# Logits and gate product at one place of a step, and five more weight blocks at the seam to the tail

## The chip, the cores and the metric

The kernel runs on one core of one Trainium2 chip. The metric is the device time of one execution in microseconds (us). The engines named below are PE (TensorE, matrix products; PEld is its weight load), DVE (VectorE), ACT (ScalarE), POOL (GpSimd) and SP (SyncE, which issues every DMA here).

## The reference

Three stages follow one another; everything is float32.

```
# 1 memory attention: 4 batches, 8 heads, 576 tokens, 64 wide, 32 memory slots
a    = softmax(phi, over tokens)                  # [4,8,576,32]
k_m  = a.T @ k ;  v_m = a.T @ v                   # [4,8,32,64]
attn = softmax(q @ k_m.T / 8) @ v_m
x    = attn, heads side by side                   # [2304,512]
# 2 experts weighted by domain: 4 experts, w1 512x1024, w2 1024x512
x    = sum_e p[:,e] * (relu(x @ w1[e]) @ w2[e])   # p = domain_probs, rows normalised
# 3 slots: 8 experts with 4 slots each
logits = x @ phi2                                 # [2304,32]
s    = softmax(logits, over tokens).T @ x         # 32 slot inputs
s    = relu(s[expert] @ v1[expert]) @ v2[expert]  # v1 512x1024, v2 1024x512
out  = softmax(logits, over slots) @ s
```

## The kernel before

The body never forms the 512-wide `x` of stage 2. Per batch it has attention weights `A` (two parts, high and low) and the product G of each head's `v_m` with `w1` (`g_mult`, L374 to L397). A hidden block is then G times A: `up()` (L424 to L449) is six matrix products of 128x128 by 128x288 (L435 to L437), a ReLU on ACT into a buffer `hT` (L445), and, after the last range of tokens, a transpose on DVE into `h` (L447). `logits()` (L451 to L472) multiplies `hT` by M, the product of `w2` and `phi2`, into the bank `lb`; its 128x32 products are line L469. `g_mult` has 64x32 products (L392), 16 of them per step into two of four PSUM banks called `at`; `g_out` (L399 to L403) takes each bank out by a cast on ACT (L402) and a subtraction on DVE (L403).

The work is cut into units: batches 0, 1 and 2 whole (two ranges of 288 tokens each), batch 3 in two halves (units 3 and 4). A unit has 8 steps n of 512 hidden columns. The 24 steps of units 0 to 2 and the two steps in which units 3 and 4 go together have eight `up` calls each (full steps); the other twelve have four. The order is written by hand: a loop over the `up` calls of a step (places 0 to 7) puts `logits` of the step before behind place `at_l`, `g_mult` of the next step behind `at_g`, `g_out` at the places `at_c`, and calls `pump()` at every place. `pump()` takes one item from the list `fg` and one from `bg`. `bg` holds the attention of a later batch. `fg` holds the stages of the unit that just ended, put there by `finish()`: `whole` (L575, L578, L579), `stats` (L586 to L594), `exps`, `weights(0)` and `weights(1)` (L615 and L617, which write `we`), then `sums` (L644, 32x32 products of `we` with `h`, into all four `at` banks; L652 or L654 adds them to `srun`), then row stages for the softmax over slots (L662 to L688). `None` in these lists is a place left empty.

The weights of stage 3 are 128x512 blocks of 256 KB, taken in one fixed order: 32 of `w2`, 64 of `v1`, 64 of `v2`. `fill` puts the next blocks into a buffer that has come free, and SP issues their DMAs, each after the one eight places ahead of it has landed. The seam is the stretch behind the last `up`: the last `logits`, `whole` to `weights` of unit 4, the last `sums`, with short products of the identity (`warm`, L790) between them that compute nothing. `warm2` takes a new `lb` bank for them. Behind the last `sums` the buffers `raw`, `g` and `A0`, which held `h` until then, take weight blocks, and the tail computes stage 3 from them.

Of the kernel before, what the change touches and what calls it, by code (L numbers as in the profile page):

```python
# [8 lines left out]
F32 = mybir.dt.float32  # L9
F32R = mybir.dt.float32r  # L10
ACTF = mybir.ActivationFunctionType
ALU = mybir.AluOpType
# [4 lines left out]
def kernel(  # L17
# [23 lines left out]
    nc = tc.nc  # L41
# [11 lines left out]
    pc = ctx.enter_context(tc.tile_pool(name="pc", bufs=1))  # L53
    hTp = ctx.enter_context(tc.tile_pool(name="hTp", bufs=5))
# [10 lines left out]
    def mbank():  # L65
        return psm.tile([128, 512], F32, tag="mm", name="mm")
# [13 lines left out]
    pe = const.tile([128, B, NT, E], F32)  # L80
# [280 lines left out]
    NU = len(units)  # L361
# [43 lines left out]
    hid, hT, half, joint = {}, {}, [None], {}  # L405

    def hid_tile(u, e):

        b, ranges = units[u]
        nt = (ranges[-1][1] - ranges[0][0]) // 32  # L410
        if u < NU - 2:
            hid[u, e] = big([128, nt, 8, 32], "h")
        elif u == NU - 2:
            if e % 2 == 0:
                half[0] = big([128, 2, nt, 8, 32], "h")
            hid[u, e] = half[0][:, e % 2]
        elif e == 0:
            hid[u, e] = const.tile([128, nt, 8, 32], F32, tag="A0", name="h")
        elif e < 3:
            hid[u, e] = rawp.tile([128, nt, 8, 32], F32, tag="raw", name="h")  # L420
        else:
            hid[u, e] = gp.tile([128, nt, 8, 32], F32, tag="g", name="h")
# [108 lines left out]
    def group(u):  # L531

        b, ranges = units[u]
        base, end = ranges[0][0], ranges[-1][1]
        w = end - base
        nt, tb0 = w // 32, base // 32
        st = {}

        def flat(t):
            return t.rearrange("p n s -> p (n s)")  # L540
# [56 lines left out]
        def exps():  # L597
# [9 lines left out]
                )  # L607
            st["zg"] = zg

        def weights(h):  # L610

            def f():
                if h == 0:
                    st["dt"] = pc.tile([128, nt, 32], F32, tag="lt", name="dt")
                    nc.vector.transpose(out=flat(st["dt"]), in_=flat(st["lc"]))  # L615
                we = st["we", h] = pc.tile([128, nt, 2, 32], F32, tag="we", bufs=2, name="we")
                nc.vector.tensor_tensor(  # L617
                    out=we, in0=st["dt"].unsqueeze(2).to_broadcast([128, nt, 2, 32]),
                    in1=pe[:, b, tb0:tb0 + nt, 2 * h:2 * h + 2].unsqueeze(3).to_broadcast(
                        [128, nt, 2, 32]  # L620
                    ), op=ALU.mult,
                )
                if h == 1:
                    nc.vector.tensor_copy(out=mrun, in_=st["mg"])
                    if st["first"]:
                        nc.vector.tensor_copy(out=zrun, in_=st["zg"])
                    else:
                        nc.vector.scalar_tensor_tensor(
                            out=zrun, in0=zrun, scalar=st["fo"], in1=st["zg"],
                            op0=ALU.mult, op1=ALU.add,  # L630
                        )
            return f
# [106 lines left out]
    def fill(pool, tag, n, again=True, **kw):  # L739

        n = min(n, len(order) - nxt[0])
        if n:
            t = pool.tile([128, n, 512], F32, tag=tag, name="v", **kw)
            keys = order[nxt[0]:nxt[0] + n]
            m = 0
            while m < n:
                m += fetch(t[:, m:n], n - m)
            left = [n]
            for key in keys:
                held[key] = (left, again, pool, tag, n, kw)  # L750
# [11 lines left out]
    with tc.manual_schedule():  # L762
# [14 lines left out]
            out=dp[:, 0:16, :].rearrange("p (b r) e -> p b (r e)", b=B),  # L777
# [7 lines left out]
        wb = [mbank()]  # L785

        def warm(n):

            for _ in range(n):
                nc.tensor.matmul(wb[0][:, 0:128], ident, ident, start=True, stop=True)  # L790
# [7 lines left out]
        for n in range(2):  # L798
            nc.gpsimd.memset(kbd[n], 0.0)
        nc.vector.tensor_reduce(  # L800
            out=si, in_=ident.rearrange("p (c s) -> p s c", c=4), axis=AX.X, op=ALU.add
        )
        for i in range(4):
            nc.vector.tensor_copy(out=rr[:, i, :], in_=si)
            nc.vector.tensor_copy(
                out=r2[:, i, :].rearrange("p (b i s) -> p b i s", b=2, i=4),
# [16 lines left out]
        def warm2(n):  # L823
            wb[0] = psl.tile([128, 512], F32, tag="lb", name="wb")
            warm(n)
# [12 lines left out]
            out=dp, in0=dp, in1=dps.unsqueeze(2).to_broadcast([128, 18, E]), op=ALU.mult  # L838
# [22 lines left out]
        fg, bg, heavy = [], [], []  # L861
# [13 lines left out]
        def attention(b, lead):  # L875
# [26 lines left out]
            return items  # L902

        groups = [group(u) for u in range(NU)]

        steps = [(n, (b,)) for b in range(B - 1) for n in range(NCH)]
# [4 lines left out]
        def finish(lu, n):  # L911

            _, g_, sums, rows = groups[lu]
            if lu < NU - 2:
                rw = [None] * 5 + [f for row in rows for f in (row, None, None)]
            else:
                rw = [f for row in rows for f in (row, None)]
            if lu < NU - 2:
                ps_ = [sums(k, 5) for k in range(5)] if lu < NU - 3 else [sums(k, 4) for k in range(4)]
                fg.extend([None] * 3 + g_[:2] + [None] + g_[2:5])  # L920
                fg.extend([None] * (2 if lu < NU - 3 else 3) + ps_ + rw)
            else:
                ps_ = [sums(k, 2) for k in range(2)]
                fg.extend([None] + g_[:5] + ps_ + [None] * 4 + rw)
            heavy[:] = [g_[0]] + ps_
            if lu < NU - 3:
                bg.extend([None] * 5 + attention(lu + 2, 5))

        for n, us in steps:
            b = units[us[0]][0]  # L930
            s = b * NCH + n
            ups = [
                (u, fb, ki) for fb in range(4) for u in us for ki in range(len(units[u][1]))
            ]
            if us == (0,) and n == 0:
                ups.sort(key=lambda x: x[2])

            if len(ups) == 8:
                at_l, at_g, at_c = 0, 2, (3, 4)
            elif n == MIX:  # L940
                at_l, at_g, at_c = 1, 2, (3,)
            else:
                at_l, at_g, at_c = int(us != (NU - 1,) or n > MIX), 0, (1, 2)
            if us == (0,) and n == 0:
                bg += attention(1, 4)
                bg.insert(12, shares)
            if n == 0 and us[0]:
                assert len(bg) == 0
            if n % 2 == 0:
                for u in us:  # L950
                    hid_tile(u, n // 2)
            if us == (NU - 2,) and n == MIX:
                fill(att, "ph", 2, again=False)
                fill(att, "kt", 1, again=False)
                fill(att, "q", 1, again=False, bufs=2)
            if us == (NU - 2,) and n == NCH - 1:
                fill(bigp, "big", 9)
            if us == (NU - 1,) and n == MIX:
                fill(gp, "g", 4)
                for _ in range(4):  # L960
                    fill(bigp, "big", 9)
            gs = []
            for at, (u, fb, ki) in enumerate(ups):
                up(u, n, fb, ki)
                if at in at_c and gs:
                    gs.pop(0)()
                    if us == (0,):
                        gs.pop(0)()
                if at == at_l:
                    for lu, ln in last:  # L970
                        logits(lu, ln)
                    for lu, ln in last:
                        if ln % 2:
                            groups[lu][0](ln // 2)
                        if ln == NCH - 1:
                            finish(lu, n)
                if at == at_g and s + 1 < NG and us != (NU - 1,):
                    gs = g_mult(s + 1)
                pump(not gs or at != at_g)
                if us == (0,):  # L980
                    for f in early[at] if n == 0 else ():
                        f()
                    if n and at in (1, 2, 3, 4, 6, 7):
                        ms[n][(1, 2, 3, 4, 6, 7).index(at) + 1]()
                    if at == 5 and n + 1 < NCH:
                        ms[n + 1][0]()
            for f in gs:
                f()
            last = [(u, n) for u in us]
# [2 lines left out]
        groups[lu][0](ln // 2)  # L992
        fill(const, "A1", 4, again=False)
        fill(const, "M", 2, again=False)

        g_ = groups[lu][1]
        warm2(8)
        g_[0]()
        for f in g_[1:]:
            f()  # L1000
        warm2(14)
        groups[lu][2](0, 1)()
        warm2(6)
        for _ in range(2):
# [30 lines left out]
        part = pc.tile([128, 512], F32, tag="acc", name="part")  # L1035
# [214 lines left out]
```

## Time and profile before

| | |
|---|---|
| time, median of 3 | 575.85 us (574.59 to 579.08) |
| the profiled execution: time / span / mean granted clock | 577.05 us / 575.3 us / 0.983 |
| PE busy | 532.0 us, 92% of the span |
| DVE busy | 288.6 us, 50% |
| ACT busy | 217.4 us, 38% |
| DMA | 106.24 MB, mean 185 GB/s |

A busy time is the sum over an engine's instructions, overlaps within the engine taken once. The granted clock is the share of full speed at which PE was run: 1.0 is 2.4 GHz. The body lasts to about 464 us of the span, the seam to about 486 us, and the tail is the rest.

### The profile page before, as it was taken

The numbers are of one execution on the slowest core, as the hardware profiler recorded it, in microseconds if no ns is written. First come the engines' busy times: TensorE is split into PE (matmuls) and PEld (weight loads), VectorE is DVE, ScalarE is ACT, GpSimd is POOL, SyncE is SP. The second block draws the span as 40 slices with busy tenths as digits, with TensorE's granted clock in tenths as the row PEclk, the third lists the DMA queues.
The fourth block names the chain that finished last, engine by engine and source line by source line (L and its number), as shares of the span: only waits on it lengthen the run. The fifth ranks groups of instructions, "written<-read, shape, count | busy, mean of one in ns | idle before, by whom it ended". The sixth has DMA issues, their size and how long they took to land.

```text
span 575.3 us, 15609 instructions
## 1 busy us (share of the span) xinstructions
PE 532.0 (92%) x6814; PEld 380.6 (66%) x6814; DVE 288.6 (50%) x612; ACT 217.4 (38%) x557; POOL 18.0 (3%) x31
## 2 busy tenths in 40 slices
PE   7989999999999899999999999998999987998983
PEld 7767777777776678867667887765676765333341
DVE  5546525544480756767256667753567461022022
ACT  2445555655551345545124455421343220011022
POOL 0000001001000010100000010000010010000000
PEclk9999999999999999999999999999999998899798
DMA  8995444444240844424067333241722597999997
GB/s 200 317 286 213 136 143 163 156 148 148 74 124 5 262 153 129 139 75 123 3 191 224 93 106 142 75 149 28 255 106 74 180 389 264 373 386 386 355 355 261
DMA packets 91492, 106.24 MB, mean 185 GB/s; under 512 B 29472, under 2 KB 54560, under 8 KB 91424
## 3 DMA queue, kind: packets, MB, share of 16 engines
q1 hardware_dynamic: 91424, 105.24, 56.3%
q8 instruction: 54, 0.88, 0.6%
q14 instruction: 14, 0.11, 0.1%
HBM read 100.50 MB, written 4.72 MB: 183 GB/s over the span
## 4 chain that ended last, share of the span: by engine, by line
PE 74%; DMA 10%; DVE 8%; issue 4%; ACT 3%; SPq 2%; POOL 0%; DVEq 0%; ACTq 0%; POOLq 0%
PE mm L435 12%; PE mm L437 10%; PE mm L436 9%; PE at L644 9%; PE lb L469 6%; PE at L392 5%; DMA v<-in_moe_w_dram 5%; PE mm L1195 4%; DMA raw<-in_moe_w_dram 3%; PE at L316 3%; PE at L496 2%; DVE g L403 2%; PE mm L790 2%; PE at L224 2%; PE at L300 1%
## 5 line engine op out<-in xcount | busy, mean ns | idle before, releaser
L445 ACT ACTIVATE hT<-mm 128x288 f32<-128x288 f32 x256 | 105.8, 414 | 206.3 <-PE mm L437 182.3
L447 DVE STREAM_TRANSPOSE h<-hT 128x576 f32<-128x576 f32 (+1 forms) x160 | 103.6, 652 | 150.5 <-ACT hT L445 137.9
L435 PE MATMUL mm<-A,g 128*128 128x288 f32 x512 | 167.2, 327 | 1.8 <-ACT g L402 1.0
L437 PE MATMUL mm<-A,g 128*128 128x288 f32 x512 | 151.5, 296 | 1.6 <-DVE g L403 1.6
L436 PE MATMUL mm<-A,g 128*128 128x288 f32 x512 | 151.1, 295 | 0.8 <-DVE A L353 0.8
L435 PEld LDWEIGHTS mm<-A,g 128*128 128x128 f32 x512 | 96.5, 189 | 46.0 <-issue 27.6
L437 PEld LDWEIGHTS mm<-A,g 128*128 128x128 f32 x512 | 96.2, 188 | 2.9 <-DVE g L403 2.9
L436 PEld LDWEIGHTS mm<-A,g 128*128 128x128 f32 x512 | 96.6, 189 | 1.2 <-DVE A L353 1.0
L644 PE MATMUL at<-h,we 32*32 32x256 f32 x2304 | 55.6, 394 | 6.7 <-issue 4.0
L644 PEld LDWEIGHTS at<-h,we 32*32 32x32 f32 x2304 | 33.6, 104 | 24.3 <-issue 9.2
L403 DVE TENSOR_TENSOR g<-at,g 128x512 fp32r<-128x512 f32 x64 | 41.7, 667 | 2.3 <-ACT g L402 2.2
L469 PE MATMUL lb<-hT,M 128*32 128x288 f32 x512 | 39.6, 413 | 0.2 <-ACT M L522 0.2
L392 PE MATMUL at<-raw,vb 64*32 64x512 f32 x512 | 35.7, 601 | 1.9 <-DMA raw<-in_moe_w_dram 1.5
L402 ACT CAST g<-at 128x512 fp32r<-128x512 f32 x64 | 36.4, 585 | 0.0
L1195 PE MATMUL mm<-v,hz 128*8 128x256 f32 x256 | 29.8, 415 | 4.1 <-DMA v<-in_moe_w_dram 3.5
L1195 PEld LDWEIGHTS mm<-v,hz 128*8 128x8 f32 x256 | 11.2, 93 | 21.1 <-DMA v<-in_moe_w_dram 9.9
L496 PE MATMUL at<-ident,w 128*128 128x128 f32 x128 | 20.0, 279 | 2.4 <-DVE g L403 2.4
L469 PEld LDWEIGHTS lb<-hT,M 128*32 128x32 f32 x512 | 13.1, 109 | 12.7 <-issue 5.6
L316 PEld LDWEIGHTS at<-kbd,qt 128*128 128x128 f32 (+1 forms) x160 | 17.8, 180 | 3.8 <-issue 3.0
L316 PE MATMUL at<-kbd,qt 128*128 128x64 f32 (+1 forms) x160 | 19.4, 264 | 0.2
L496 PEld LDWEIGHTS at<-ident,w 128*128 128x128 f32 x128 | 14.5, 141 | 6.5 <-DVE g L403 3.4
L1055 PE MATMUL mm<-v,sT 128*32 128x512 f32 x128 | 16.3, 653 | 1.1 <-DMA v<-in_moe_w_dram 0.8
(159 smaller groups left out, 489.8 us busy)
## 6 DMA issues: line engine op xcount, KB each, us to landing
raw<-in_moe_w_dram SPq DMA_DIRECT2D x32, 1024.0 KB, 5.2
v<-in_moe_w_dram SPq DMA_DIRECT2D x18, 1024.0 KB, 13.8
v<-in_moe_w_dram SPq DMA_DIRECT2D x46, 256.0 KB, 6.0
w<-in_moe_w_dram SPq DMA_DIRECT2D x16, 512.0 KB, 6.9
v<-in_moe_w_dram SPq DMA_DIRECT2D x10, 768.0 KB, 10.5
kv<-in_k_dram SPq DMA_DIRECT2D x8, 512.0 KB, 5.1
kv<-in_v_dram SPq DMA_DIRECT2D x8, 512.0 KB, 6.0
out_dram<-ot SPq DMA_DIRECT2D x16, 256.0 KB, 4.1
```

The source lines that it names most:

```text
L316: nc.tensor.matmul(sc[0:n, :, j, :], st["qt"][:, j, 0:n], kbd[b % 2][:, j], start=True, stop=True)
L392: nc.tensor.matmul(ts[c][32 * i:32 * i + 32, :], vb[b % 2][64 * c:64 * c + 64, 32 * i:32 * i + 32], raw[s][64 * c:64 * c + 64, i, :], star ...
L403: nc.vector.tensor_tensor(out=lo, in0=t, in1=hi.bitcast(F32), op=ALU.subtract)
L435: nc.tensor.matmul(ps, gh, ah, start=(c == 0), stop=False)
L436: nc.tensor.matmul(ps, gh, al, start=False, stop=False)
L437: nc.tensor.matmul(ps, gl, ah, start=False, stop=(c == 1))
L445: nc.scalar.activation(out=t[:, o0 - base:o1 - base], in_=ps, func=ACTF.Relu)
L447: nc.vector.transpose(out=hid[u, n // 2][:, :, 4 * (n % 2) + fb], in_=t[:, 0:o1 - base])
L469: nc.tensor.matmul(lb[0][p:p + 32, 0:o1 - o0], M[:, 4 * n + a, :], hT[u, n, a][:, o0 - base:o1 - base], start=start, stop=stop,)
L496: nc.tensor.transpose(t[:, 128 * c:128 * c + 128], st["w"][:, a, 128 * c:128 * c + 128], ident)
L644: nc.tensor.matmul(ts[p][32 * e:32 * e + 32, 0:256], st["we", e // 2][rows, tb, e % 2], hid[u, e][rows, tb].rearrange("p k f -> p (k f)"), ...
L1195: nc.tensor.matmul(accs[acc][32 * i:32 * i + 8, 0:256], hz[:, dh != 2, f, i, :], blk[:, 256 * m:256 * m + 256], start=(dh == 2 and f == 0) ...
```

## The change

- In 24 of the 26 full steps (not in steps 0 and 1 of unit 0) `logits` and `g_mult` both stand behind the second `up`, and the two parts of `g_out` at places 2 and 3.
- Of units 0 to 2 the stages from `whole` on begin one place earlier, and the first `sums` stand two places earlier than before in the list; counted in places of the step the first one is at place 4 instead of 5 (unit 2: 5 instead of 6). Of units 3 and 4 the row stages come two places earlier.
- The last unit writes its weights `we` in two halves of token tiles, both expert pairs of a half together.
- At the seam the five `hT` buffers take one weight block each, ahead of everything that `raw`, `g` and `A0` take.
- The `warm` products use a bank of `up`, not `lb`, and are 4 and 10, not 8 and 14.

```diff
+        def part(h, t0, n):
+            if t0 == 0:
+                st["we", h] = pc.tile([128, nt, 2, 32], F32, tag="we", bufs=2, name="we")
+            nc.vector.tensor_tensor(
+                out=st["we", h][:, t0:t0 + n],
...
         def weights(h):
...
-                we = st["we", h] = pc.tile([128, nt, 2, 32], F32, tag="we", bufs=2, name="we")
-                nc.vector.tensor_tensor(
...
+                if u < NU - 1:
+                    part(h, 0, nt)
+                else:
+                    for g in range(2):
+                        part(g, 5 * h, 5 if h == 0 else nt - 5)
...
-                fg.extend([None] * 3 + g_[:2] + [None] + g_[2:5])
-                fg.extend([None] * (2 if lu < NU - 3 else 3) + ps_ + rw)
+                fg.extend([None] * 2 + g_[:2] + [None] + g_[2:5])
+                fg.extend([None] * (1 if lu < NU - 3 else 2) + ps_ + rw)
...
-                fg.extend([None] + g_[:5] + ps_ + [None] * 4 + rw)
+                fg.extend([None] + g_[:5] + ps_ + [None] * 2 + rw)
...
-                at_l, at_g, at_c = 0, 2, (3, 4)
+                at_l, at_g, at_c = (0, 2, (3, 4)) if us == (0,) and n < 2 else (1, 1, (2, 3))
...
         fill(const, "M", 2, again=False)
+        for _ in range(5):
+            fill(hTp, "hT", 1, again=False)
...
-        warm2(8)
+        wb[0] = mbank()
+        warm(4)
...
-        warm2(14)
+        wb[0] = mbank()
+        warm(10)
```

The order of instructions, as the program issues them. On PE, in a full step of unit 0 during which another batch's attention runs (L224 to L263 are its work), before:

```order
L437 MATMUL mm<-A_97,g 128x288
L469 MATMUL lb<-hT,M 32x288 x8
L244 MATMUL at<-ind,sm 128x1
L248 MATMUL at<-ind,ph 128x1
L244 MATMUL at<-ind,sm 128x1
L248 MATMUL at<-ind,ph 128x1
L435 MATMUL mm<-A_97,g 128x288
...
L392 MATMUL at<-raw,vb_101 32x512 x8
L263 MATMUL at<-ident,km 128x128
```

and now:

```order
L437 MATMUL mm<-A_97,g 128x288
L469 MATMUL lb<-hT,M 32x288 x8
L392 MATMUL at<-raw,vb_101 32x512 x8
L244 MATMUL at<-ind,sm 128x1
L248 MATMUL at<-ind,ph 128x1
L244 MATMUL at<-ind,sm 128x1
L248 MATMUL at<-ind,ph 128x1
L435 MATMUL mm<-A_97,g 128x288
```

L469 and L392 were two interruptions of the `up` products and are one.

On DVE, in step 1 of unit 1, where unit 0's weights are written and its first sums follow (in the changed kernel the weights are line L614 for L617, `mrun` and `zrun` L634 and L636), before:

```order
L617 TENSOR_TENSOR we<-dt,pe 128x1152
L447 STREAM_TRANSPOSE h<-hT 128x18x32
L617 TENSOR_TENSOR we<-dt,pe 128x1152
L624 COPY mrun<-mg 128x1
L626 COPY zrun<-zg 128x1
L447 STREAM_TRANSPOSE h<-hT 128x18x32
L403 TENSOR_TENSOR g<-at,g 128x512 x2
L447 STREAM_TRANSPOSE h<-hT 128x18x32 x2
```

and now:

```order
L614 TENSOR_TENSOR we<-dt,pe 128x1152
L447 STREAM_TRANSPOSE h<-hT 128x18x32
L403 TENSOR_TENSOR g<-at,g 128x512
L614 TENSOR_TENSOR we<-dt,pe 128x1152
L634 COPY mrun<-mg 128x1
L636 COPY zrun<-zg 128x1
L447 STREAM_TRANSPOSE h<-hT 128x18x32
L403 TENSOR_TENSOR g<-at,g 128x512
L447 STREAM_TRANSPOSE h<-hT 128x18x32 x2
```

The two subtractions that free G's banks stand apart, one ahead of the second weights and one behind them.

On SP, at the seam (all of these are loads of weight blocks), before:

```order
L717 DMA v<-in_moe_w_dram 128x512
L717 DMA v<-in_moe_w_dram 128x2x512
L717 DMA v<-in_moe_w_dram 128x512
L717 DMA v<-in_moe_w_dram 128x3x512
L717 DMA v<-in_moe_w_dram 128x512
L717 DMA v<-in_moe_w_dram 128x3x512
```

and now:

```order
L727 DMA v<-in_moe_w_dram 128x512
L727 DMA v<-in_moe_w_dram 128x2x512
L727 DMA v<-in_moe_w_dram 128x512 x5
L727 DMA v<-in_moe_w_dram 128x4x512 x6
```

Five single blocks (the `hT` buffers) stand ahead of the first load into `raw`.

## Rows read from the trace of the kernel before

**Rows 1.** The page: busy time by engine, the chain that ended last by engine.
```profile
PE 532.0 (92%) x6814; PEld 380.6 (66%) x6814; DVE 288.6 (50%) x612; ACT 217.4 (38%) x557; POOL 18.0 (3%) x31
...
PE 74%; DMA 10%; DVE 8%; issue 4%; ACT 3%; SPq 2%; POOL 0%; DVEq 0%; ACTq 0%; POOLq 0%
```

**Rows 2.** Timeline, PE, full step of unit 1: start, duration, instruction, [idle before, releaser].
```profile
257.43 0.29 PE L437 MATMUL mm<-A,g 128*128 128x288 f32 x1
257.66 1.18 PE L469 MATMUL lb<-hT,M 128*32 128x288 f32 x16
258.76 0.40 PE L435 MATMUL mm<-A,g 128*128 128x288 f32 x1
259.00 0.29 PE L436 MATMUL mm<-A,g 128*128 128x288 f32 x1
```

**Rows 3.** Timeline, PE: logits with sums right behind them.
```profile
181.18 1.18 PE L469 MATMUL lb<-hT,M 128*32 128x288 f32 x16
182.28 2.75 PE L644 MATMUL at<-h,we 32*32 32x256 f32 x128
```

**Rows 4.** Timeline, all engines, around unit 0's first sums.
```profile
168.10 1.32 DVE L617 TENSOR_TENSOR we<-dt,pe 128x1152 f32<-128x1152 f32 x1
170.15 1.25 DVE L403 TENSOR_TENSOR g<-at,g 128x512 fp32r<-128x512 f32 x2
170.29 3.23 PE L644 MATMUL at<-h,we 32*32 32x256 f32 x96
171.45 1.59 PEld L644 LDWEIGHTS at<-h,we 32*32 32x32 f32 x90 [0.47 <-DVE g L403]
173.46 0.40 PE L435 MATMUL mm<-A,g 128*128 128x288 f32 x1
```

**Rows 5.** Timeline, PE: sums of the same size without a wait.
```profile
178.13 2.12 PE L644 MATMUL at<-h,we 32*32 32x256 f32 x96
180.19 0.40 PE L435 MATMUL mm<-A,g 128*128 128x288 f32 x1
```

**Rows 6.** Timeline, PE: waits in full steps, one row of each kind.
```profile
88.98 0.66 PE L496 MATMUL at<-ident,w 128*128 128x128 f32 x4 [0.54 <-DVE g L403]
...
189.86 1.42 PE L392 MATMUL at<-raw,vb 64*32 64x512 f32 x16 [0.15 <-DVE srun L652]
195.08 0.33 PE L173 MATMUL at<-ident,mx 128*128 128x128 f32 x1 [1.01 <-DVE mx L160]
201.71 1.09 PE L392 MATMUL at<-raw,vb 64*32 64x512 f32 x16 [0.74 <-DMA raw<-in_moe_w_dram]
254.84 0.31 PE L347 MATMUL at<-ident,ex 64*128 64x64 f32 x2 [1.37 <-DVE ex L339]
```

**Rows 7.** Windows: from:to, us, busy (count) of PE PEld DVE ACT POOL, PEclk, DMA share, GB/s.
```profile
470.00:480.00 10.00, 7.63 (x228) 5.78 (x228) 3.34 (x9) 1.19 (x4) 0.00 (x0) 1.00 1.05 388
480.00:492.00 12.00, 10.16 (x147) 5.50 (x150) 2.58 (x7) 0.59 (x1) 0.00 (x0) 0.86 0.69 220
492.00:520.00 28.00, 25.47 (x200) 9.05 (x192) 5.88 (x27) 4.07 (x7) 0.00 (x0) 0.94 1.05 388
```

**Rows 8.** Timeline, PE and DVE, the seam.
```profile
463.88 1.24 PE L469 MATMUL lb<-hT,M 128*32 128x288 f32 x8
466.48 2.05 PE L790 MATMUL wb<-ident 128*128 128x128 f32 x16 [1.35 <-DVE lt L551]
473.78 4.62 PE L644 MATMUL at<-h,we 32*32 32x256 f32 x201 [0.77 <-DVE we L617]
481.33 3.31 PE L644 MATMUL at<-h,we 32*32 32x256 f32 x87 [2.93 <-issue]
...
465.94 0.48 DVE L551 STREAM_TRANSPOSE lt<-lb 128x288 f32<-128x288 f32 x1
...
472.97 1.43 DVE L617 TENSOR_TENSOR we<-dt,pe 128x576 f32<-128x576 f32 x2
```

**Rows 9.** Windows: the sums behind the 2.93 us stop alone.
```profile
481.40:484.50 3.10, 3.10 (x87) 1.84 (x86) 0.00 (x0) 0.00 (x0) 0.00 (x0) 0.51 0.26 97
```

More of the change, by code (lines that the diff above doesn't have):

```diff
@@ L608, in exps @@
             st["zg"] = zg
+        def part(h, t0, n):
[3 more added lines that the diff above has]
+                out=st["we", h][:, t0:t0 + n],
+                in0=st["dt"][:, t0:t0 + n].unsqueeze(2).to_broadcast([128, n, 2, 32]),
+                in1=pe[:, b, tb0 + t0:tb0 + t0 + n, 2 * h:2 * h + 2].unsqueeze(3).to_broadcast(
+                    [128, n, 2, 32]
+                ), op=ALU.mult,
+            )
         def weights(h):
@@ L615, in f @@
                     nc.vector.transpose(out=flat(st["dt"]), in_=flat(st["lc"]))
-                we = st["we", h] = pc.tile([128, nt, 2, 32], F32, tag="we", bufs=2, name="we")
-                nc.vector.tensor_tensor(
[L618 to L622, printed above, removed]
+                if u < NU - 1:
[3 more added lines that the diff above has]
+                        part(g, 5 * h, 5 if h == 0 else nt - 5)
                 if h == 1:
```

## The prediction

> **What bounds the kernel now.** The page comes first: PE is busy 92% of the span and has 74% of the chain that ended last, DMA 10%, DVE 8%, issue 4% [rows 1]. So in the body an edit is worth what it takes off PE's own stream, and a DVE edit counts only where PE waits for DVE. The second view is PE's timeline in a full step: how far the starts of its products lie apart where it leaves the `up` stream and returns. The third is the list of PE's waits, with the DVE rows beside each. The last is the DMA rate in windows from the seam on: 388 GB/s in 470 to 480 and in 492 to 520, but 220 GB/s in 480 to 492 [rows 7]. There the loads set the tail, and the hole in them is what can be won.
>
> All sums are made against the profiled execution (577.05 us), which is 1.2 us above the median of 575.85; differences are applied to the median.
>
> **One place for logits and G.** Inside a run of `up` products PE starts one every 0.13 us (259.00 is followed at that distance). From the last L437 to the first L469 it is 257.66 - 257.43 = 0.23, so leaving costs about 0.10; the first L435 on return starts 0.24 ahead of the next product, again some 0.10 more than 0.13 [rows 2]. An interruption costs about 0.19 in all (0.09 and 0.10 as the mean of several such places). In the order of PE's instructions the `up` stream is left 165 times before and 149 times now: the 24 changed steps save one each, and the moved attention and sums give some back. 16 x 0.19 = 3.0; in three of these steps the first sums wait for DVE anyway, which swallows it there. I take -2.7.
>
> That the passage from L469 to L392 inside the merged place is free is an assumption: no row of before has that pair. The nearest is L469 followed by L644, two shapes that differ more: start to start 182.28 - 181.18 = 1.10 for 16 products [rows 3], and L469 followed by L435 has 258.76 - 257.66 = 1.10 as well [rows 2]. No gap shows. The bounds are -3.0 (free) and about -1.3 (an extra 0.1 in each of 16 places). Against it, the Trainium skill ("TensorEngine Tiling (Array Packing)", Key Properties) says that a change of tiling mode drains TensorE; by it 128x32 to 64x32 would cost again what leaving the stream costs and the term would be near -1.4. The rows just named do not show such a drain.
>
> **The first sums of a unit.** They take all four `at` banks, so they wait until DVE has taken G out of the last two. Before, unit 0's first sums start at 170.29 but run 3.23 us, where the same 96 products take 2.12 without a wait [rows 4, 5]: 1.1 us lost, until DVE's second L403 ends at 171.40 (170.15 + 1.25). Ahead of it DVE has been busy without a break with `dt`, 1.36 and 1.32 for `we`, and two transposes [rows 4]. The change puts the first sums one `up` earlier: 0.80 us of PE work (six products at 0.13) that used to cover this wait now stands behind it. DVE's work up to the second L403 is the same list in another order (one L403 ahead of the second `we`), so it ends at the same time at best; the banks of the second L403 come free later by up to one L403 (0.63) if the first is delayed by its cast. So each of the units 0 and 1 loses between 0 (if DVE's chain, whose first item also stands one place earlier, starts earlier by as much) and 1.4 (0.80 + 0.63). I take 1.4 for both, since DVE has no idle time there [rows 4] to start earlier in, and 0.8 for unit 2 in the joint steps: +3.6, with PE standing some 2.8 us at such a place. Bounds 0 and +4.2.
>
> **Other waits that move.** One row of each kind is shown [rows 6]; twins elsewhere have about the same size. Gone: unit 0's flips (L496) that wait for L403, 0.54 and two of 0.43, since G's banks are free two places earlier (-1.2, one of them kept in part); G's wait for `raw`, 0.74 and a twin of 0.76 (-1.5): the raw tile is let go earlier in the step before, so its load starts earlier; G's wait for `srun`, 0.15 and 0.33 stretched (1.42 instead of 1.09), twice (-1.0): the sums now end a place earlier; part of L347's 1.37, twice (-0.7). Grown: L173 waits for L160, which now stands behind both L403 on DVE, so 1.01 becomes some 2.0, twice (+2.0); a like delay for the next attention stage, 0.3 twice (+0.6). Together -1.8; bounds -4.4 (nothing grows) and +2.6 (nothing goes).
>
> SP's stream in the body holds the `raw` loads only a place earlier; nothing that PE waits for is queued behind them. ACT is at 38% [rows 1] and gets no work. POOL is untouched.
>
> **The seam and the tail.** In 480 to 492 the loads ran at 220 GB/s, on both sides at 388 [rows 7]. 12 x (388 - 220) / 388 = 5.2 us of loading is missing: SP had issued all it could, and the next buffers (`raw`, `g`, `A0`) come free only when the last sums end at 484.6 (481.33 + 3.31) [rows 8]. Now five blocks more, 5 x 0.262 MB = 1.31 MB or 3.4 us at 388 GB/s, are ready before. The queue empties about 3.4 us later, near 484.7 instead of 481.3. The seam itself gets shorter: row stages of unit 4 that DVE has ahead of the L551 at 465.94 move earlier (0.9), `warm` no longer waits 1.35 for the `lb` bank and is half as long (2.05 to about 1.0), and half of the 1.43 for `we` comes after the first sums can start (0.7) [rows 8]. Some of that overlaps: 2 to 2.8 us. The last sums then end near 482, before the queue is empty, and the hole closes but for the latency of the first new load. Behind it the loads set the pace, 388 in 492 to 520 [rows 7], so what the loads win the end wins: I take -4.7, with bounds 0 and -5.2. The `hT` blocks keep `hT` from the ReLU of stage 3 for a while, about 0.3 us, which the loads hide; if they did not, it would cost 0.3.
>
> **Sum.** -2.7 + 3.6 - 1.8 - 4.7 = -5.6, and 575.85 - 5.6 = **570.2 us**. Own range 567.5 to 572.5.
>
> **Rivals.**
> - *The clock falls at the first sums.* After 2.93 us of idle time the sums at 481.4 to 484.5 ran at a granted clock of 0.51 [rows 9], the 1.2 GHz level, and took 3.31/87 = 0.038 us each, where the 201 before took 4.62/201 = 0.023 [rows 8]. The stop that I forecast at first sums is as long (2.8). Against it, PE is densely busy ahead of these places. About 3.2 us at the low level cost 1.3; two units: 572.8. Chance 0.18.
> - *The stop of 2.93 us "issue" grows with the queue.* PE waited for nothing in the program, and it went on at 481.33, when the load queue had run dry. If it ends only when the loads do, the longer queue holds the sums, and so `raw`, until 484.7, and the hole merely moves: the tail gives 0.5 instead of 4.7, and the time is 574.5. For it: the coincidence. Against it, a single case. The Trainium skill ("DMA: Bandwidth & Descriptors", Queues, rings and completion order) says that a DMA engine takes its queues in turn, packet by packet, by which a fetch would not wait for all the loads; no run here shows that. Chance 0.11.
> - *DVE's chain starts earlier with its stages and nothing is lost at first sums* (0 for +3.6), and the hole closes wholly: 565.8. Chance 0.18.
> - *The merged place pays for the change of shape*, 0.1 in each: 571.5. Chance 0.05.
> - *Slower.* The stops at the first sums bring the low clock, as in the first rival, and it stays: at 0.038 for 0.023 each us there loses 0.4 us of work. The gains are worth 5.6, so it decides from 14 us at the low level in all, or 4.7 us behind each of three stops; 8 to 12 us behind each lose 9.6 to 14.4, which gives 580 to 584.5. Against it, a granted clock of 0.983 over the span, with waits of over 1 us in the body already. Chance 0.10.
>
> That the change does not do what it says is excluded by the order of the instructions.
>
> **How the numbers follow.** My forecast has the remaining 0.38. One per cent, about what a measurement of this kernel can tell from no change, is 5.8 us: 570.1 and 581.6. Faster by more: half of the forecast (0.19), all of 565.8 (0.18), and the edges of the others (0.04): 0.41. Slower by more: half of the slow rival, 0.05. Within: 0.54. The range 564.5 to 576 takes in all cases but the slow one (0.10) and the tails of the others (under 0.10).
>
> **What would show it.** In the profile after: L469 followed by L392 at 1.10 from start to start (a longer distance: the fifth case); first sums of units 0 and 1 waiting about 2.8 us for L403, with the clock at 1.0 behind them (lower: the first rival; about 1.1 us as before: the third); no wait for `raw` at G, and about 2 us at L173; GB/s near 388 in every window from 470 to 520 (a hole that has only moved, with an "issue" stop at L644: the second). The prediction is wrong if PE shows waits in full steps that none of these lines names.

## The result, and the profile after

The changed kernel takes 569.38 us (median of 10 runs) against 576.63 us (10 runs) for the kernel before: ratio 0.9879, 95% interval 0.9855 to 0.9902, or 7.0 us less (5.7 to 8.4). The profiled execution takes 571.1 us with a span of 569.3 us at a mean granted clock of 0.979.

The page, the lines that answer to [rows 1]:

```profile
PE 526.9 (93%) x6798; PEld 379.6 (67%) x6798; DVE 290.0 (51%) x614; ACT 214.3 (38%) x557; POOL 17.8 (3%) x31
...
PE 72%; DMA 11%; DVE 9%; issue 3%; ACT 3%; SPq 1%; POOL 0%; DVEq 0%; POOLq 0%; ACTq 0%
```

The work is the same but for 16 products of `warm`. PE's busy time is 5.1 us shorter; no run shows how that divides among the places in the order, the stretches at the lower clock and the 16 products.

PE's timeline in step 1 of unit 1, the merged place (as in [rows 2]: start, duration, instruction):

```profile
163.35 0.29 PE L437 MATMUL mm<-A,g 128*128 128x288 f32 x1
163.58 1.18 PE L469 MATMUL lb<-hT,M 128*32 128x288 f32 x16
164.69 1.09 PE L392 MATMUL at<-raw,vb 64*32 64x512 f32 x16
165.70 0.40 PE L435 MATMUL mm<-A,g 128*128 128x288 f32 x1
165.94 0.30 PE L436 MATMUL mm<-A,g 128*128 128x288 f32 x1
```

From L469 to L392 it is 1.11 us, start to start, where L469 to L435 took 1.10 in [rows 2]: the passage from one shape to the other costs nothing that can be seen. One departure (0.23) and one return (0.24) are left.

The first sums of unit 0, PE and then DVE, answering to [rows 4]:

```profile
168.29 0.86 PE L654 MATMUL at<-h,we 32*32 32x256 f32 x6
171.19 1.20 PE L654 MATMUL at<-h,we 32*32 32x256 f32 x44 [2.04 <-DVE g L403]
```

```profile
166.40 0.78 DVE L447 STREAM_TRANSPOSE h<-hT 128x576 f32<-128x576 f32 x1
167.79 0.69 DVE L403 TENSOR_TENSOR g<-at,g 128x512 fp32r<-128x512 f32 x1 [0.62 <-ACT g L402]
168.40 1.35 DVE L614 TENSOR_TENSOR we<-dt,pe 128x1152 f32<-128x1152 f32 x1
169.66 0.15 DVE L634 COPY mrun<-mg 128x1 f32<-128x1 f32 x1
169.72 0.14 DVE L636 COPY zrun<-zg 128x1 f32<-128x1 f32 x1
169.79 0.77 DVE L447 STREAM_TRANSPOSE h<-hT 128x576 f32<-128x576 f32 x1
170.48 0.65 DVE L403 TENSOR_TENSOR g<-at,g 128x512 fp32r<-128x512 f32 x1
```

Six products run and then PE stands until DVE's second L403 ends at 171.13: 171.19 less 168.42 (168.29 and six at 0.022) is a stop of 2.8 us, 2.04 of which the trace counts as idle. DVE is not full: it waits 0.62 us for a cast, with the second weights (1.35 us, ready to run) queued behind the waiting L403.

PE's waits by what ended them (total us, times, longest):

```profile
PE at L654 <- DVE g L403: 5.4, 3, 2.1
PE at L654 <- issue: 3.6, 2, 3.1
...
PE mm L437 <- DVE g L403: 2.6, 5, 1.2
PE at L173 <- DVE mx L160: 2.5, 4, 0.6
PE at L347 <- DVE ex L339: 1.9, 3, 0.9
...
PE at L496 <- DVE g L403: 1.0, 1, 1.0
```

The same list of the kernel before has 0.6, 4.0, 1.6, 2.0, 3.0 and 2.4 for these six. Windows over the seam, answering to [rows 7] and [rows 9]:

```profile
470.00:480.00 10.00, 5.98 (x287) 4.53 (x288) 2.14 (x7) 0.06 (x1) 0.00 (x0) 1.00 1.05 386
480.00:492.00 12.00, 11.00 (x103) 5.21 (x93) 2.58 (x7) 1.17 (x2) 0.00 (x0) 1.00 1.05 385
492.00:520.00 28.00, 25.81 (x218) 9.37 (x217) 7.26 (x30) 4.68 (x9) 0.00 (x0) 1.00 1.05 387
478.60:480.50 1.90, 1.90 (x72) 1.19 (x72) 0.32 (x1) 0.00 (x0) 0.00 (x0) 1.00 1.05 384
```

The hole (220 GB/s in 480 to 492) is gone. The seam on PE, answering to [rows 8]:

```profile
463.70 1.24 PE L469 MATMUL lb<-hT,M 128*32 128x288 f32 x8
464.87 1.16 PE L800 MATMUL mm<-ident 128*128 128x128 f32 x8
...
470.96 4.58 PE L654 MATMUL at<-h,we 32*32 32x256 f32 x217 [1.34 <-DVE we L614]
478.60 1.91 PE L654 MATMUL at<-h,we 32*32 32x256 f32 x71 [3.05 <-issue]
```

The last sums end at 480.5 instead of 484.6. The body behind its first step (first `up` of step 1 of unit 0 to the first of the last step, from PE's timeline) takes 411.1 us instead of 412.5. Each of these is one execution: in the runs below this stretch takes 410.3 (the body alone) and 409.5 (the change without the blocks) with the changed order, and 411.4 (the blocks alone) with the order of before.

### The profile page after: what moved, and what is told of

Read it like the earlier page. It is cut to its first block, busy times and chain, and to the rows that moved or that the text cites. A ratio compares the mean times of both kernels' runs of the same rounds, so it can differ in the third digit from the quotient of the medians.

```text
span 569.3 us, 15570 instructions
## 1 busy us (share of the span) xinstructions
PE 526.9 (93%) x6798; PEld 379.6 (67%) x6798; DVE 290.0 (51%) x614; ACT 214.3 (38%) x557; POOL 17.8 (3%) x31
## 4 chain that ended last, share of the span: by engine, by line
PE 72%; DMA 11%; DVE 9%; issue 3%; ACT 3%; SPq 1%; POOL 0%; DVEq 0%; POOLq 0%; ACTq 0%
PE mm L435 12%; PE mm L437 10%; PE mm L436 9%; PE at L654 9%; DMA v<-in_moe_w_dram 8%; PE lb L469 5%; PE at L392 5%; DMA raw<-in_moe_w_dram 3%; PE at L316 3%; PE at L496 3%; DVE g L403 2%; PE mm L800 2%; PE at L224 2%; PE at L300 1%; DVE h L447 1%
## 5 line engine op out<-in xcount | busy, mean ns | idle before, releaser
L435 PE MATMUL mm<-A,g 128*128 128x288 f32 x512 | 165.5, 323 | 1.9 <-ACT g L402 1.0
L437 PE MATMUL mm<-A,g 128*128 128x288 f32 x512 | 151.6, 296 | 2.6 <-DVE g L403 2.6
L435 PEld LDWEIGHTS mm<-A,g 128*128 128x128 f32 x512 | 96.5, 189 | 35.9 <-issue 28.9
L437 PEld LDWEIGHTS mm<-A,g 128*128 128x128 f32 x512 | 96.4, 188 | 3.9 <-DVE g L403 3.9
L654 PE MATMUL at<-h,we 32*32 32x256 f32 x2304 | 54.2, 385 | 12.0 <-DVE g L403 5.4
L403 DVE TENSOR_TENSOR g<-at,g 128x512 fp32r<-128x512 f32 x64 | 42.5, 676 | 35.3 <-ACT g L402 35.2
L469 PE MATMUL lb<-hT,M 128*32 128x288 f32 x512 | 39.5, 413 | 0.0
L392 PE MATMUL at<-raw,vb 64*32 64x512 f32 x512 | 34.9, 601 | 0.5 <-DMA raw<-in_moe_w_dram 0.5
L496 PE MATMUL at<-ident,w 128*128 128x128 f32 x128 | 20.5, 284 | 1.1 <-DVE g L403 1.0
L469 PEld LDWEIGHTS lb<-hT,M 128*32 128x32 f32 x512 | 12.9, 109 | 12.4 <-issue 5.6
L501 ACT COPY w2T<-at 128x256 f32<-128x256 f32 x32 | 12.6, 394 | 16.4 <-PE at L496 16.3
L321 DVE TENSOR_REDUCE amx<-at 128x8 f32<-128x256 f32 (+1 forms) x20 | 8.2, 409 | 20.7 <-PE at L316 20.7
```

Source lines behind the costliest of these rows:

```text
L392: nc.tensor.matmul(ts[c][32 * i:32 * i + 32, :], vb[b % 2][64 * c:64 * c + 64, 32 * i:32 * i + 32], raw[s][64 * c:64 * c + 64, i, :], star ...
L403: nc.vector.tensor_tensor(out=lo, in0=t, in1=hi.bitcast(F32), op=ALU.subtract)
L435: nc.tensor.matmul(ps, gh, ah, start=(c == 0), stop=False)
L437: nc.tensor.matmul(ps, gl, ah, start=False, stop=(c == 1))
L469: nc.tensor.matmul(lb[0][p:p + 32, 0:o1 - o0], M[:, 4 * n + a, :], hT[u, n, a][:, o0 - base:o1 - base], start=start, stop=stop,)
L496: nc.tensor.transpose(t[:, 128 * c:128 * c + 128], st["w"][:, a, 128 * c:128 * c + 128], ident)
```

## The experiments

**The body alone, the seam alone.** The kernel before with one or the other part of the diff.

```diff
 body:  at_l, at_g, at_c and the lists of units 0 to 2 as in the change; nothing else
 seam:  hT blocks, warm, part(), "+ [None] * 2 + rw" of units 3 and 4; nothing else
```

> The kernel before with the body's part of the change alone: logits and G at one place, and the lists of units 0 to 2; seam and tail as before. Theory (the body breaks even: what the 24 merged places save is lost again to waits for DVE, at the first sums above all; the profile of the changed kernel begins its last step 0.18 us earlier than before): -0.2 us, between -1.5 and +1. Rival (the body gives the 2.7 us that I forecast for the merged places and more, and the profiles hide it by chance): -3 us or more. In the profile: first sums of units 0 and 1 with 2.0 to 2.1 us of wait for L403, and the hole of 5 us in the loads at 480 to 492 still there.

Measured: ratio 0.9989 (0.9972 to 1.0006), -0.6 us, so the rival (-3 us or more) falls; the hole is there (236 GB/s in 480 to 492), and the three first sums wait 5.4 us in all. The first product of stage 3 over `v1` (L1055) waits 2.9 us for weight blocks in this run, 0.8 in the kernel before: part of what the body wins may be lost again in the hole, which no run tests.

> The kernel before with the seam's part of the change alone: five hT blocks, warm in an up bank and shorter, the last weights in halves, the row stages of units 3 and 4 earlier; body as before. Theory (the whole gain is the hole in the loads): -5.5 to -7 us. Rival (body and seam share it): -4 us. In the profile: loads at 385 to 389 GB/s in every window from 460 to 520.

Measured: 0.9908 (0.9891 to 0.9925), -5.3 us; 387 GB/s in 470 to 480, 368 in 480 to 492. The point lies just below the range that the theory gave, and its interval (-6.3 to -4.3) clear of the rival's 4.0. The seam has most of the gain, the body next to none. Together they make 5.9 of the 7.0; the rest is inside the intervals.

**The five blocks alone, and the change without them.**

```diff
 before, with:   +        for _ in range(5):
                 +            fill(hTp, "hT", 1, again=False)
 change, without the same two lines
```

> The kernel before with the five hT blocks alone (1.31 MB, 3.4 us of loading at 388 GB/s); the seam keeps its length, the last sums end near 484.6. Theory (the tail is as late as its loads; the hole of 5.2 us gets 3.4 us of work): -3.4 us, between -2.5 and -4.5. Rival A (the shorter seam does it, the blocks are loaded early but nobody waits for them): 0 to -1. Rival B (the stop 'issue' in the last sums lasts until the queue of loads is empty): the stop begins at the same place, near 478.4, but lasts 6 instead of 2.9 us, and the gain is below 0.5 us.

Measured: 0.9934 (0.9914 to 0.9954), -3.8 us. Windows and PE's timeline of this run:

```profile
470.00:480.00 10.00, 7.67 (x229) 5.81 (x228) 3.34 (x9) 1.21 (x4) 0.00 (x0) 1.00 1.05 387
480.00:492.00 12.00, 10.14 (x159) 5.25 (x162) 2.58 (x7) 0.59 (x1) 0.00 (x0) 1.00 1.04 372
```

```profile
473.82 4.62 PE L644 MATMUL at<-h,we 32*32 32x256 f32 x201 [0.77 <-DVE we L617]
481.40 2.05 PE L644 MATMUL at<-h,we 32*32 32x256 f32 x87 [2.96 <-issue]
```

The seam is as long as before up to 481.40, yet the hole shrank from 5.2 to 12 x (388 - 372) / 388 = 0.5 us. The blocks are 3.4 us of loading; the rest fits the last sums, which ran at the full clock in this execution and ended at 483.45 instead of 484.64. The "issue" stop ended at the same place after 2.96 us, with loads running at 382 to 389 GB/s from 478 to 484: it does not wait for the queue to empty. Rivals A and B both fall.

> The changed kernel without the five hT blocks: only the shorter seam feeds the hole. Theory: raw, g and A0 come free near 480.4 instead of 484.6, some 4 us earlier, while the queue runs dry near 481: the hole closes nearly all the same, -4 to -5.5 us against the kernel before, so that blocks and shorter seam do not add up (alone -3.4 and about -4.5, together -6). Rival A of the run before: all of the change, -7. Rival (the two add, blocks worth what they are worth alone): 3.4 us less than the change, about -3.8 with the hole of 3.4 us in the loads.

Measured: 0.9932 (0.9906 to 0.9959), -3.9 us. The theory expected the hole nearly closed. It is not, and the second rival (the two add) comes closest:

```profile
470.00:480.00 10.00, 6.95 (x192) 5.01 (x183) 1.88 (x6) 0.00 (x0) 0.00 (x0) 0.83 0.90 324
480.00:492.00 12.00, 10.62 (x97) 4.20 (x99) 1.80 (x4) 1.17 (x2) 0.00 (x0) 1.00 0.95 320
```

A hole of 10 x (388 - 324) / 388 + 12 x (388 - 320) / 388 = 3.8 us is left. The last sums end 2.7 us earlier after the last `up` than before (18.9 us behind its start, not 21.6), not 4: in this execution they ran at the low clock again (71 products in 3.15 us, 1.91 in the profile above). The hole does not ask how long the seam is but when the buffers come free against when loading began, and it began 0.8 us earlier too (12.9 us ahead of the last `up`, not 12.0). So blocks and shorter seam nearly add: 3.8 and about 1.5 (-5.3 less -3.8). One figure does not fit well: body alone (0.6) and shorter seam (1.5) would make 2.1, and this run, which is the two together, has 3.9 (2.4 to 5.4).

**Where the body's gain went.** Step by step (distance from the first `up` of a step to that of a later one), change less before: unit 0, steps 2 to 7, -1.99 us; steps 4 to 7 of units 1 and 2, -1.12 and -1.14; steps 0 to 3 of these units, where the first sums stand, +0.38 and +0.90; the joint steps with the first step of four `up` calls behind them -0.18; all later steps of four calls, which the merge does not touch, +1.79. Two of these rest on one execution: steps 0 to 3 of unit 2 took 57.09 us in the change but 56.31 and 56.19 in the two other runs with its body, and the first step of four took 14.76 before but 13.65 in the run with the blocks alone, whose body is the same. So +0.90 may be near +0.2 and -0.18 near +0.5. The other figures repeat in those runs to within 0.3. The +1.79 nobody had forecast. There two `up` calls wait for G's bank. PE and DVE of the changed kernel in the first of the two steps:

```profile
413.68 0.40 PE L437 MATMUL mm<-A,g 128*128 128x288 f32 x1 [1.17 <-DVE g L403]
```

```profile
410.95 0.69 DVE L403 TENSOR_TENSOR g<-at,g 128x512 fp32r<-128x512 f32 x1
411.56 0.47 DVE L551 STREAM_TRANSPOSE lt<-lb 128x288 f32<-128x288 f32 x1
411.95 0.71 DVE L672 TENSOR_REDUCE cmx<-lr 128x18 f32<-128x576 f32 x1
412.58 0.47 DVE L447 STREAM_TRANSPOSE h<-hT 128x288 f32<-128x288 f32 x1
412.97 0.65 DVE L403 TENSOR_TENSOR g<-at,g 128x512 fp32r<-128x512 f32 x1
```

L672, a row stage of unit 2, stands ahead of the second L403. In the kernel before, the row stage (L662 there) stood behind that L403, and the wait was 0.51:

```profile
414.29 0.65 DVE L403 TENSOR_TENSOR g<-at,g 128x512 fp32r<-128x512 f32 x1
414.86 0.73 DVE L662 TENSOR_REDUCE cmx<-lr 128x18 f32<-128x576 f32 x1
```

It moved because the sums ahead of it in the list did.

```diff
-                rw = [None] * 5 + [f for row in rows for f in (row, None, None)]
+                rw = [None] * (5 if lu < NU - 3 else 6) + [f for row in rows for f in (row, None, None)]
```

> The changed kernel, but the row stages of unit 2 one place later (one None more ahead of them), as they stood before the change. Theory (in two steps of unit 3 the moved row stages, 0.71 and 0.75 us on DVE, stand ahead of the subtraction that frees G, and PE waits 1.17 and 0.82 for it where it waited 0.51 and 0.19): those two waits return to about 0.5 and 0.2 and the time falls by 1.3 us against the changed kernel (ratio to before 0.9856 instead of 0.9879). Rival (the waits come from the earlier sums of unit 2, not from its row stages): waits and time as in the changed kernel.

Measured: 0.9856 (0.9824 to 0.9889), 567.63 us. The waits are back at the sizes of before, and the steps of four `up` calls (from the second on) take 57.9 us again, as before and 1.8 less than in the change:

```profile
410.19 0.40 PE L437 MATMUL mm<-A,g 128*128 128x288 f32 x1 [0.51 <-DVE g L403]
...
415.92 0.40 PE L437 MATMUL mm<-A,g 128*128 128x288 f32 x1 [0.19 <-DVE g L403]
```

The cause is shown by these rows; the time against the change (1.3 us) lies within the two intervals.

**The first sums.** The next two runs act on the wait of 2.0 us, from DVE's side and from PE's.

```diff
 chain earlier
-                fg.extend([None] * 2 + g_[:2] + [None] + g_[2:5])
-                fg.extend([None] * (1 if lu < NU - 3 else 2) + ps_ + rw)
+                fg.extend([None] * 1 + g_[:2] + [None] + g_[2:5])
+                fg.extend([None] * (2 if lu < NU - 3 else 3) + ps_ + rw)
 four portions
-                ps_ = [sums(k, 5) for k in range(5)] if lu < NU - 3 else [sums(k, 4) for k in range(4)]
+                ps_ = [sums(k, 4) for k in range(4)]
-                fg.extend([None] * (1 if lu < NU - 3 else 2) + ps_ + rw)
+                fg.extend([None] * 2 + ps_ + rw)
```

> The changed kernel, but whole, stats, exps and the weights of units 0 to 2 one place earlier, the first sums where they are. DVE then has the second weights ahead of both subtractions and starts its chain 0.8 us earlier. Theory (the first sums wait for DVE's chain, which had been held back by idle gaps of 0.83, 0.25 and 0.62 us and not by its own work alone): the wait at the first sums of units 0 and 1 falls from 2.04 and 2.10 to about 0.5, the time by 3 us against the changed kernel (ratio to before 0.983). Rival (DVE is full there, the order of its list does not matter): waits of 2 us as before, no gain. Second rival (transposes and subtractions pushed back by the weights now hold PE at its up products): the first sums wait less, but PE waits 1 us or more at L435 to L437 in the same steps.

Measured: 0.9855 (0.982 to 0.989), 567.41 us. First sums of unit 0 on PE, and DVE ahead of them:

```profile
166.99 0.88 PE L654 MATMUL at<-h,we 32*32 32x256 f32 x6
168.51 1.86 PE L654 MATMUL at<-h,we 32*32 32x256 f32 x79 [0.64 <-DVE g L403]
```

```profile
163.19 2.63 DVE L614 TENSOR_TENSOR we<-dt,pe 128x1152 f32<-128x1152 f32 x2
...
166.55 0.65 DVE L403 TENSOR_TENSOR g<-at,g 128x512 fp32r<-128x512 f32 x1
167.12 0.76 DVE L447 STREAM_TRANSPOSE h<-hT 128x576 f32<-128x576 f32 x1
167.81 0.65 DVE L403 TENSOR_TENSOR g<-at,g 128x512 fp32r<-128x512 f32 x1
```

Both weights now run without a gap ahead of the subtractions, and the wait is 0.64. That DVE was full falls; so does the second rival (L435 to L437 wait no longer than in the change). The body took 407.4 us in this execution, 3.7 less than in the profile of the change and 2.1 less than in the run without the blocks, which has the same body as the change; the time shows 1.4 us, less than the 3 expected, in intervals that overlap.

> The changed kernel, but the sums of units 0 and 1 in four portions instead of five, from place 5 on instead of place 4 (unit 2: unchanged). Theory (the wait at the first sums is the time that an up of 0.8 us used to cover): it falls from 2.04 and 2.10 to about 1.2, and one interruption of 0.19 less per unit: -2 us against the changed kernel (ratio to before 0.9845). Rival (the last subtraction is itself delayed when PE goes on, as its cast queues behind one more ReLU on ACT): the wait stays at 2, the time within 0.5 us of the changed kernel.

Measured: 0.9966 (0.9937 to 0.9996), 575.55 us: 5 us slower than the change, which neither theory had. The first sums do wait less (1.6 for 2.1 at the longest), but elsewhere a wait has grown:

```profile
195.20 0.33 PE L173 MATMUL at<-ident,mx 128*128 128x128 f32 x1 [1.86 <-DVE mx L160]
```

A stage of `heavy` holds back the attention's list `bg` at its place; with one such stage fewer, that list ran one place ahead, into other company on DVE. The waits are not all of it. Behind two of the longer ones the granted clock fell to the lower level: behind 1.65 us at L347 (until 253.85) and behind 1.85 us at L173 (until 301.17). The two windows:

```profile
254.74:258.15 3.41, 3.41 (x17) 3.41 (x16) 0.94 (x2) 0.82 (x2) 0.00 (x0) 0.50 0.00 0
302.53:305.94 3.41, 3.41 (x17) 3.39 (x16) 1.83 (x4) 1.04 (x3) 0.00 (x0) 0.50 1.05 386
```

This is the mechanism of the prediction's first rival, at another place. It does not come every time: behind the twin waits at L173 (until 195.20) and L347 (until 361.39) the clock stayed at 1.00. All three edits together, before this was seen:

> The changed kernel with the three edits of this call together: row stages of unit 2 later, the chain of units 0 to 2 one place earlier, four portions of sums for units 0 and 1 (first sums of unit 2 unchanged). Theory: no wait above 0.3 us at the first sums of units 0 and 1; the waits worth 2.0, 2.1 and 1.3 us go, and 0.4 us of interruptions: -5.5 us against the changed kernel (ratio to before 0.978). Rival (the tail's loads set the end by themselves, an earlier body only waits longer for them): gain below 2 us, with longer waits for weight blocks in the tail.

Measured: 0.9897 (0.9865 to 0.9929), 570.12 us: the two good edits give back what the third loses. No long wait is left at the first sums (0.6 at most), L173 waits 4.1 us in all, and the clock fell twice in the body here as well (193.9 to 197.3 and 255.4 to 258.8, granted 0.50). The rival foresaw that little is gained, but its reason does not hold: PE waits 3.7 us for weight blocks in the two large products of stage 3, 3.2 in the change, 0.5 more where 5.5 us were to be explained.

**The list put back in its place.**

```diff
-                bg.extend([None] * 5 + attention(lu + 2, 5))
+                bg.extend([None] * 6 + attention(lu + 2, 5))
```

> The kernel with four portions of sums (which came out near the kernel before, 0.9966), with one None more ahead of the attention of the later batch, so that its stages stand in the places of the changed kernel again. Theory (four portions let the other list, that of the attention, run one place ahead, and its maxima L160 then wait on DVE behind the sums' additions: L173 1.86 us twice, L347 1.7): L173 waits at most 0.7 and L347 at most 0.9 again, and the time is 1 us below the changed kernel (ratio 0.986). Rival (four portions cost by themselves, longer stretches of sums in which DVE and ACT run dry): 0.996 as without the None.

Measured: 0.9843 (0.9811 to 0.9875), 567.34 us. One `None` is worth 7 us; the waits of L173 are those of the change again, and the rival falls:

```profile
PE at L173 <- DVE mx L160: 2.5, 4, 0.6
PE at L347 <- DVE ex L339: 1.9, 3, 0.9
```

The body behind its first step takes 407.9 us instead of 415.0. About half of the 7.1 us is the waits and half the clock: without the `None`, steps 2 and 3 of unit 1 and step 7 of unit 2, with a longer wait alone, took 0.9 us more each time; steps 2 and 3 of unit 2 (2.7 more) and step 7 of unit 1 with the step behind it (2.4 more) had the lower clock besides. With the `None` the clock does not fall in the body at all in the profiled execution, and over all executions the mean granted clock is 0.985 to 0.991 with the `None` and 0.965 to 0.983 without it.

> The changed kernel with the two edits that each gained: row stages of unit 2 one place later, and the chain from whole to the weights of units 0 to 2 one place earlier. Theory (the two take away different waits of PE): first sums wait 0.6 us instead of 2.0, the two steps of unit 3 wait 0.5 and 0.2 for L403 instead of 1.17 and 0.82, and the gains add: -3.5 us against the changed kernel (ratio to before 0.982). Rival (the tail's loads take back what the body gains): no better than either edit alone, 0.9855.

Measured: 0.9849 (0.9819 to 0.9879), 567.55 us, no better by time than either edit alone. Its profiled execution has a span of 562.5 us and all the waits that the theory foresaw (0.6 at the first sums, 0.5 at L437), but the median does not bear it out. The body of that execution fits a sum (405.5 us, against 407.4 with the earlier chain and 408.3 with the later rows). It is the fastest of the six and the one with the highest mean granted clock (0.988; 0.975 to 0.986 in the others), so the clock as well as the tail may take something back; which of them does stays open.

> The changed kernel with all four edits: rows of unit 2 later, chain of units 0 to 2 earlier, four portions of sums, attention's list one place later. Theory: all gains together, no wait above 0.3 us at the first sums of units 0 and 1, L173 as in the changed kernel: -4.5 us against it (ratio to before 0.980). Rival (once DVE is in time at the first sums, the extra up ahead of them only moves: as the two edits alone, 0.982).

Measured: 0.9793 (0.9761 to 0.9826), 564.43 us, 11.9 less than the kernel before and clear of the change's interval. This is the fastest version of the study. The wait at unit 1's first sums is still 0.6 us, not below 0.3. The rival's 0.982 lies inside the interval, and the interval of the two edits alone (0.9819 to 0.9879) touches it, so that the last two edits add something on top is likely but not shown.

## Why the prediction was right, point by point

- **The time.** 570.2 forecast, 569.38 measured; a gain of 5.6 forecast, 7.0 measured (5.7 to 8.4). The times lie closer than the gains because the forecast starts from 575.85 and the kernel before took 576.63 beside the change.
- **The merged place, -2.7.** Plain full steps lost 0.18 to 0.21 us each (step 0 of unit 1 9.84 to 9.64, the first joint step 9.76 to 9.55): the 0.19 of the working, and 16 of them make the 3.0. The fourth rival (the change of shape costs) falls by the 1.11 us from L469 to L392.
- **The first sums, +3.6.** The stop came out at 2.8 us where 2.8 was forecast, and the third, in the joint steps, at 1.29 us of idle time. The reason was half wrong. The prediction and the description of the change say that the stages from `whole` on come one place earlier. In the list they do; but `finish()` now runs behind place 1 and not 0, so in the step `whole` to the first weights stand where they stood, and the second weights one place later, behind a waiting L403. So the third rival had no ground in this change. Run "chain earlier" is what it described, and there the wait fell to 0.64.
- **Other waits, -1.8.** Too dark for L173 (a growth of 2.0 forecast; it went from 2.0 to 2.5, so 0.5), about right for L496 (2.4 to 1.0) and L347 (3.0 to 1.9), too bright for `raw` (1.5 to 0.5). Missing altogether: unit 2's row stages, +1.3 in two waits, 1.8 over their steps. These are steps of four calls, and the prediction looked for unforeseen waits in full steps only. With them the body came to -0.6 (-1.6 to +0.35) where my terms gave -0.9. That the two agree is luck in part: 1.5 too much for L173 and 1.8 left out nearly cancel.
- **Seam and tail, -4.7.** -5.3 (-6.3 to -4.3) measured with the seam alone, by the mechanism named: the hole closes, and mostly by the five blocks (3.8 alone, for 3.4 us of loading). From the start of the last `up` to the end of the last sums it is 3.95 us less than before; with the seam alone, where the last sums ran at the low clock as before, it is 2.6, within the 2 to 2.8 of the forecast.
- **The first rival (low clock at the first sums)**: the granted clock behind the stop is 1.00 (171 to 176), and it stays there through the rest of the body. But the lower clock did come behind shorter waits (1.65 and 1.85 us) in the run with four portions, so the rival named a real cost. **The second (the stop waits for the queue)**: 2.96 us with the queue running. **The slow one**: no sign of it.

## What to carry to other kernels

A loader that stands empty while compute still holds its buffers is worth about its hole (here 5.2 us, and 5.3 us were won when it closed): divide the missing bytes by the rate on either side, and look for a few buffers that come free sooner. When stages are placed by lists that pace one another, an edit to one list moves the others; list for each engine which instruction now stands ahead of the one that frees a bank, in every step and not only in those the edit is about. One empty place was worth 7 us here, half of it through waits and half through the lower clock behind them.

## What the runs showed of the hardware

The first step, which no run changes, takes 18.6 us in eight of the thirteen profiled executions (the kernel before among them) and 20.1 in five (the change among them). In the longer ones PE is granted the lower of its two levels for a while, after a start with the same instructions. The window from 30 to 34 us, before and then after:

```profile
30.00:34.00 4.00, 4.00 (x35) 3.53 (x36) 1.06 (x5) 2.03 (x6) 0.00 (x0) 1.00 1.08 322
```

```profile
30.00:34.00 4.00, 4.00 (x23) 3.61 (x22) 0.90 (x4) 1.69 (x5) 0.00 (x0) 0.59 1.07 313
```

So the profiled execution of the change is 6.0 us faster than that of before (571.1 and 577.05) in spite of 1.5 us lost there. The same happens at the last sums behind the "issue" stop: clock 0.51 before and low in the run without blocks and with the seam alone, 1.00 in the change and with the blocks alone. A single profile carries 1 to 2 us of this, which is why bodies are compared here from the second step on. The "issue" stop itself lasts 2.8 to 3.4 us in every run. It keeps its place in PE's stream of instructions, not in the sums: in all thirteen traces it stands behind the first 6171 to 6176 products of PE, so that with 16 `warm` products fewer it comes behind 217 of the last sums instead of 201. In each of them one packet of 16 KB on the DMA queue that the page calls "q8 instruction" starts 0.3 to 0.7 us behind the beginning of the stop (at 478.91 before, 476.10 in the change), and PE goes on 2.3 to 2.6 us after that start. So PE most likely stands there until its next instructions are loaded; no run varied that load by itself.
